# An eight-expert MLP behind an FFT filter: the seven products in another order, and transfers moved to ScalarE's queue

## The chip, the cores and the metric

The kernel runs on one core of one Trainium2 chip. The metric is the time of one execution in microseconds on the device. In the profile the engines are PE (TensorE, matmuls) with PEld (its weight loads), DVE (VectorE), ACT (ScalarE), POOL (GpSimd) and SP (SyncE, which issues transfers). A transfer is issued by an engine's queue, in that queue's order, and is then moved by the 16 DMA engines. `L808` is line 808 of the kernel before.

## The reference, cut to what matters

Two blocks follow each other. The first filters every one of 8 sequences of 2496 rows and 256 channels along the sequence; the second sends every row through one of eight two-layer networks, chosen by a hash of its token number.

```python
def _attn_ref(x, filt_r, filt_i):          # x: (8, 2496, 256)
    X = np.fft.rfft(x, axis=1)
    F = (filt_r + 1j * filt_i)[None, :, :]
    return np.fft.irfft(X * F, n=x.shape[1], axis=1).astype(np.float32)

def _moe_ref(x, token_ids, w1, w2):        # x: (19968, 256), w1: (8, 256, 1024), w2: (8, 1024, 256)
    expert_idx = token_ids * np.int64(2654435761) % np.int64(8)
    for e in range(8):
        mask = expert_idx == e
        h = np.maximum(x[mask] @ w1[e], 0.0)
        out[mask] = h @ w2[e]
```

All values are float32.

## The kernel before

**The filter.** The transform over 2496 = 39 x 64 points is done as two small transforms. A batch goes through four steps: `stage1` (L239) multiplies by a table over 39 points and writes a block to memory (`d1`), `load2` (L258) reads it back turned, `forward` (L266) does the second transform on PE and multiplies by the filter on DVE (tiles `y` and `z` from a pool of three buffers with the tag "p"), `back` (L285) transforms back and writes `d2`, `load4` (L362) reads that, and `stage3` (L367) ends the transform and scatters the finished rows with indirect transfers into a buffer `xs` in memory, ordered by expert. The writes of `d1` (L256) and `d2` (L301) are issued from POOL, except those of batch 2's `d1`, which are issued from ACT. The first two batches are handled in the head of the kernel in another way, on the chip alone.

**The tiles.** `xs` is cut into tiles of 256 rows, each belonging to one expert. There are 85 places for tiles; 80 (`NSURE`) are always computed, the last five only if the count of used tiles asks for it, behind a branch (`rest`, L902). With the given inputs the profile shows 80 down products (2560 matmuls of 32 each), so the five were not computed. A tile can start when all batches that may hold its rows are scattered; five stages (`STAGES`, after 2, 3, 4, 6 and 8 batches) say so, and the tiles start at 0, 10, 20, 30 and 50. A row of `xs` holds 256 channels and four words with its row number in the output.

**One tile** (`step`, L869) issues in this order: the load of the tile after next (`load`, L754: four transfers on SP, each of 64 channels, the last one a word wider so that the row number comes along); `numbers` (L769) for the next tile, four small copies on POOL that pick the row numbers out of the loaded rows; `weight_sums` (L792) for the next tile, four subtractions on POOL; the scatter of the last tile's results (`store`, L848, two indirect transfers on POOL); `up`; the next weights of the up product; the next tile's tokens, transposed and summed on DVE (`token_parts`, `token_sums`); then `down` (L836), 32 matmuls for the second layer, and its next weights. Between `up` and `down`, at three places within `down`, and after it, `run_until` issues the pieces of the filter for later batches that fall due, by a written list of times in units of a tile.

**`up` (L801)** forms the first layer with seven products of half size instead of eight, in three banks of PSUM, a, b and c. A product is four matmuls of 128 columns (eight records in the profile). The order is a, c, b, a, b, c, b, and a second or third product on a bank adds to what stands there. Sums that leave a bank are taken by DVE (`plus`, L815, 0.69 us) and by ACT (a copy of the first a, L819; relus, L812). A product that adds to b or c once more must wait until DVE has read the bank; each further product has its own reader.

**The head** counts tokens by expert (`count` to `experts`), and a list of times below zero sets its order. `weights` for tiles 0 and 1 go through SP at times -99 to -98.7; `begin` (L746) at -76 closes the head's work area and loads tiles 0 and 1, half of the transfers on SP and half on ACT. `blanks` works out, at -80, the places in `xs` that hold no token, and `pads` (L639) at 7.4 writes empty rows there: 14 indirect transfers (`NQP`) from one buffer of the pool with the tag "p".

Transfers from SP and ACT share eight completion counters, which the program gives out in turn, so that the issue of one waits until the one before it on its counter has landed. Indirect transfers and others from POOL have eight of their own.

Of the kernel before, what the change touches and what calls it, by code (L numbers as in the profile page):

```python
# [19 lines left out]
P = 128  # L20
# [14 lines left out]
SG = 4  # L35
# [18 lines left out]

XW = C // 4 + 2

# [63 lines left out]
def kernel(  # L120
# [60 lines left out]
    class Batch:  # L181
# [57 lines left out]
        def stage1(self, u):  # L239
# [7 lines left out]
            if half == 1:  # L247


                eng = nc.scalar if self.b == 2 else nc.gpsimd  # L250
                moves = self.parts(self.d1, self.t1, v)
                if self.b == 2 and v > 0:
                    put_off.extend(moves)
                    return
                for dram, chip in moves:
                    eng.dma_start(out=dram, in_=chip)  # L256

# [27 lines left out]
        def back(self, u):  # L285
# [12 lines left out]
            if u % half == half - 1:  # L298
                for p in range(2):
                    a0 = p * NS + SG * (u // half)  # L300
                    nc.gpsimd.dma_start(out=self.d2[:, a0:a0 + SG, :],  # L301
                                        in_=self.g[p:P:2, :, :])
# [94 lines left out]
    def weights(i, which):  # L397
# [3 lines left out]
        if i >= 2 and which == 0:  # L401
            ws[i] = ws[i - 2][0:2]
        eng, kw = nc.sync, {}
        if which == 0:
# [233 lines left out]

    def pads():  # L639
        blank = ppool.tile([P, 2 * C], I32, name="blank", tag="p")[:, 0:W]  # L640
        nc.vector.memset(blank[:, 0:C], 0)
        nc.vector.memset(blank[:, C:], N)
        for q in range(NQP):
            scatter(blank.bitcast(F32), at_i[:, q:q + 1], "xs_pad")
# [57 lines left out]
    todo += [(-154.2, count), (-152, route), (-150.9, later)]  # L702
    todo += [(-137.2, places), (-128, tile_experts), (-121, experts), (-80, blanks), (7.4, pads)]
    todo += [(t, lambda k=k: spread_filters(k)) for k, t in enumerate((-150.45, -146.6, -143, -137.6))]
# [8 lines left out]
    todo += [(t, lambda v=v: batches[2].load1(v)) for v, t in enumerate((-119, -117.5, -116))]  # L713
    todo += [(t, lambda u=u: batches[2].stage1(u)) for u, t in enumerate((-101.5, -99.5, -86, -85.5, -85, -84.5))]

    todo += [(-75.5, lambda: [nc.scalar.dma_start(out=dram, in_=chip) for dram, chip in put_off])]
    todo += [(t, lambda k=k: weights(k // 2, k % 2)) for k, t in enumerate((-99, -98.9, -98.8, -98.7))]
    todo += [(-76, lambda: begin())]

# [34 lines left out]
    def load(i):  # L754

        g = gath.tile([P, TB // 32, XW], F32, name=f"xg_{i}", tag="xg")
        rows = xs[tiles[i] * TB:(tiles[i] + 1) * TB, :]
        for q in range(4):
            w = C // 4 + (q == 3)
            ld = (nc.scalar if i < 2 and q % 2 else nc.sync).dma_start(  # L760
                out=g[32 * q:32 * q + 32, :, 0:w], in_=rows[:, 64 * q:64 * q + w].rearrange("(a t) c -> t a c", t=32))
            for b in range(STAGES[stage_of[i]], B):
                tc.declare_no_dep(ld.ins, group=f"xs_{b}", reason="the tiles of a stage hold tokens of its batches alone")
            if stage_of[i] < G - 1:
                tc.declare_no_dep(ld.ins, group="xs_pad", reason="places without a token lie in the last stage alone")
            tc.add_to_no_dep_group("xs_read", ld.ins)
        xg[i] = g

    def numbers(i):  # L769

        no = nums.tile([P, 2], I32, name=f"no_{i}", tag="no")
        for a in range(4):
            nc.gpsimd.tensor_copy(no[32 * a:32 * a + 32, :], xg[i][96:128, a::4, C // 4].bitcast(I32))  # L773
        to_rows[i] = no

# [24 lines left out]

    def up(i, ht):  # L801
        w1, x, st, t = ws[i][0], parts[i], parts[i]["sums"], sums[i]
        ps = {k: banks[k].tile([P, 4, P], F32, name=f"up_{i}_{k}", tag=k) for k in "abc"}
        h11, h12, h21, h22 = [ht[:, h, 4 * f:4 * f + 4, :] for h in range(2) for f in range(2)]

        def product(bank, w, xx, first):
            for f in range(4):
                nc.tensor.matmul(out=ps[bank][:, f, :], lhsT=w[:, f * P:(f + 1) * P], rhs=xx,  # L808
# [9 lines left out]
        product("a", w1[:, 0, 0:h], x[0, 0], True)  # L818
        nc.scalar.copy(out=h21, in_=ps["a"][:])  # L819
        product("c", t[0], st[:, 0, :], True)  # L820
        plus(h22, "c", h21)
        product("b", t[1], st[:, 1, :], True)
        plus(h12, "b", h21)
        product("a", w1[:, 1, 0:h], x[0, 1], False)
        relu(h11, ps["a"][:])
        product("b", t[2], st[:, 2, :], False)
        plus(h22, "b", h22)
        relu(h22, h22)
        product("c", w1[:, 1, h:], st[:, 3, :], False)
        plus(h12, "c", h12)  # L830
# [30 lines left out]
    weight_sums(0, nc.vector)  # L861
    numbers(0)
    used = []
# [5 lines left out]
    def step(i):  # L869
        ht = work.tile([P, 2, FP, P], F32, name=f"ht_{i}", tag="ht")  # L870
        if i + 2 < NT:
            load(i + 2)
        if i + 1 < NSURE:
            numbers(i + 1)
            weight_sums(i + 1)
        if i > 0:
            store(i - 1)
        up(i, ht)
        weights(i + 2, 0)
# [15 lines left out]
    for i in range(NSURE, NT):  # L895
        token_parts(i, mid[:, i - NSURE, 0:2 * TB].rearrange("p (d h t) -> p d h t", d=DP, h=2))
        numbers(i)
        if i + 2 < NT:
# [45 lines left out]
```

## Time and profile before

| | |
|---|---|
| median of 20 runs | 1554.39 us (1548.92 to 1558.11) |
| the profiled execution's own time | 1551.48 us |
| its span, from the first to the last instruction | 1549.8 us |
| mean granted TensorE clock | 0.969 |
| busy: PE, DVE, ACT, POOL | 1440.2, 807.2, 415.8, 894.9 us |
| longest waits: POOL's number copies (L773) | 80.9 us for out scatters, 74.5 for xs scatters, 44.5 for xg |
| POOL's writes of `d2` (L301) | 34.6 us of issue, 70.8 us of waits before them |
| POOL's writes of `d1` (L256) | 17.7 us of issue, 22.1 us of waits before them |
| number copies on POOL | 340, 64.2 us busy |

The profile is of one execution. Busy shares are means over stages with different limits: a head of about 165 us, a mixed part in which tiles and the filter of later batches alternate (to about 1069 us), a last part of tiles alone (to about 1525 us), and the end. A group's line gives the engine, the operation, what it writes and reads, how often, and its busy time; a wait's line says who waited for whom, how long in all, how often, and the longest. The matmuls' ends are modelled, so a product's cost is read from the start of one to the start of the next.

### The profile page before, as it was taken

To read this page: it belongs to the slowest core of one execution; us is meant where nothing else is said; L and a number is where in the kernel's file an instruction comes from. 1 tells how busy PE (TensorE), PEld (TensorE's weight loads), DVE (VectorE), ACT (ScalarE), POOL (GpSimd) and SP (SyncE) were. 2 spreads that over 40 slices of the span, in tenths; PEclk is the share of its full clock that TensorE was granted. 3 is DMA by queue.
4 is the path that set the end of the run, shared out by engine and by line. 5 is a ranking of instruction groups with operands and counts; after the bars stand their busy time and mean duration, and the time that the engine had idled before them with its cause. 6 is when DMAs were issued, how large, how long until landed. Compare 5 with 4: busy or idle time off the path is not lost.

```text
span 1549.8 us, 24884 instructions
## 1 busy us (share of the span) xinstructions
PE 1440.2 (93%) x8746; PEld 1296.6 (84%) x8746; DVE 807.2 (52%) x1362; ACT 415.8 (27%) x710; POOL 894.9 (58%) x1120
## 2 busy tenths in 40 slices
PE   6978799887999999999999999999999999999993
PEld 6966688776888888887998998988999999999993
DVE  6852563355456557434664456454454555545452
ACT  3543133222223323322233222222222222222220
POOL 5055436665556656657656677566765646465541
PEclk9998799898999999999999999999999999999997
DMA  8254666835897597797755653646513242332311
GB/s 225 64 179 125 176 198 184 254 110 179 254 262 233 161 286 217 236 272 250 225 159 145 181 165 112 153 132 195 150 47 112 67 123 65 99 92 69 106 42 38
DMA packets 201673, 245.73 MB, mean 159 GB/s; under 512 B 105749, under 2 KB 170701, under 8 KB 194426
## 3 DMA queue, kind: packets, MB, share of 16 engines
q1 hardware_dynamic: 168919, 166.72, 38.9%
q0 software_dynamic: 28480, 73.44, 14.5%
q10 hardware_dynamic: 4147, 3.95, 0.9%
q8 instruction: 72, 1.18, 0.3%
q14 instruction: 55, 0.45, 0.1%
HBM read 251.19 MB, written 75.14 MB: 211 GB/s over the span
## 4 chain that ended last, share of the span: by engine, by line
PE 78%; issue 6%; DMA 5%; DVE 5%; POOL 3%; another core or an unknown queue 1%; ACT 0%; SPq 0%; ACTq 0%; POOLq 0%; DVEq 0%
PE dps L841 31%; PE up_b L808 14%; PE up_c L808 8%; PE up_a L808 8%; PE pd L226 4%; PE pb L271 4%; PE pa L226 3%; PE pc L294 3%; DVE z L281 1%; DMA wts<-in_x_dram 1%; DMA xs<-o,sidx 1%; DVE ht L815 1%; POOL tw L798 1%; DMA mid<-d 1%
## 5 line engine op out<-in xcount | busy, mean ns | idle before, releaser
L841 PE MATMUL dps<-wts,ht 128*128 128x256 f32 x2560 | 582.5, 381 | 0.0
L841 PEld LDWEIGHTS dps<-wts,ht 128*128 128x128 f32 x2560 | 484.2, 191 | 66.6 <-issue 1.6
L815 DVE TENSOR_TENSOR ht<-up_b,ht 128x512 f32<-128x512 f32 x240 | 166.0, 692 | 173.1 <-PE up_b L808 134.7
L384 POOL DMA_INDIRECT xs<-o,sidx x176 | 178.1, 1012 | 128.6 <-issue 48.6
L798 POOL TENSOR_TENSOR tw<-wts 128x512 f32<-128x512 f32 x158 | 203.5, 1288 | 38.0 <-DMA wts<-in_moe_w_dram 32.1
L851 POOL DMA_INDIRECT out_dram<-osb,no x160 | 161.3, 1008 | 109.6 <-DVE osb L846 75.1
L798 POOL TENSOR_TENSOR tw<-wts,tw 128x512 f32<-128x512 f32 x158 | 204.1, 1292 | 6.2
L808 PE MATMUL up_b<-st,tw 128*128 128x128 f32 x1280 | 178.6, 284 | 31.0 <-DVE ht L815 30.6
L812 ACT ACTIVATE ht<-ht 128x512 f32<-128x512 f32 x240 | 151.1, 630 | 180.1 <-DVE ht L815 162.1
L808 PEld LDWEIGHTS up_b<-st,tw 128*128 128x128 f32 x1280 | 158.7, 195 | 43.0 <-POOL tw L798 16.7
L773 POOL COPY no<-xg 32x2 int32<-32x2 int32 x340 | 64.2, 189 | 224.6 <-DMA out_dram<-osb,no 80.9
L846 DVE COPY osb<-dps 128x512 f32<-128x512 f32 x80 | 55.4, 692 | 261.3 <-PE dps L841 226.5
L808 PE MATMUL up_a<-xt,wts 128*128 128x128 f32 x1280 | 171.3, 278 | 6.0 <-issue 6.0
L815 DVE TENSOR_TENSOR ht<-up_c,ht 128x512 f32<-128x512 f32 x160 | 110.6, 691 | 126.7 <-PE up_c L808 111.1
L808 PEld LDWEIGHTS up_a<-xt,wts 128*128 128x128 f32 x1280 | 164.0, 194 | 11.3 <-issue 7.3
L819 ACT COPY ht<-up_a 128x512 f32<-128x512 f32 x80 | 46.9, 587 | 350.4 <-PE up_a L808 340.3
L281 DVE TENSOR_TENSOR z<-pb,filt 64x512 f32<-64x512 f32 x160 | 110.2, 688 | 24.8 <-PE pc L294 22.8
L808 PE MATMUL up_b<-xt,tw 128*128 128x128 f32 x640 | 92.6, 289 | 9.2 <-DVE ht L815 7.0
L812 ACT ACTIVATE ht<-up_a 128x512 f32<-128x512 f32 x80 | 47.8, 597 | 197.0 <-PE up_a L808 146.4
L808 PEld LDWEIGHTS up_b<-xt,tw 128*128 128x128 f32 x640 | 79.8, 196 | 20.4 <-issue 10.3
L789 DVE TENSOR_TENSOR st<-xt 128x128 f32<-128x128 f32 x160 | 87.9, 550 | 2.8
L808 PE MATMUL up_c<-st,tw 128*128 128x128 f32 x640 | 85.6, 277 | 4.0 <-POOL tw L798 4.0
(145 smaller groups left out, 1483.7 us busy)
## 6 DMA issues: line engine op xcount, KB each, us to landing
wts<-in_moe_w_dram SPq DMA_DIRECT2D x162, 1024.0 KB
xg<-xs SPq DMA_DIRECT2D x253, 64.0 KB
mid<-d SPq DMA_DIRECT2D x60, 256.0 KB
d<-mid POOLq DMA_DIRECT2D x60, 256.0 KB
t<-d SPq DMA_DIRECT2D x12, 960.0 KB
x<-in_x_dram SPq DMA_DIRECT2D x36, 312.0 KB
d<-mid POOLq DMA_DIRECT2D x10, 960.0 KB
xg<-xs SPq DMA_DIRECT2D x83, 65.0 KB
```

Source lines behind the costliest of these rows:

```text
L226: nc.tensor.matmul(out=ps[0:cols * H, k, :], lhsT=w[:], rhs=src[:, 2 * i + k, :], start=True, stop=True)
L271: nc.tensor.matmul(out=ps[:, i, :], lhsT=d_t[:, s, :], rhs=rhs, start=True, stop=True)
L281: nc.vector.tensor_tensor(out=z[b], in0=ps[a], in1=f_t[1][64 * hi:64 * hi + 64, s1:s1 + 2, :], op=OP.mult)
L384: st = nc.gpsimd.indirect_dma_start(out=xs[:], out_offset=bass.IndirectOffsetOnAxis(ap=index, axis=0), in_=rows, in_offset=None, bounds_ch ...
L773: nc.gpsimd.tensor_copy(no[32 * a:32 * a + 32, :], xg[i][96:128, a::4, C // 4].bitcast(I32))
L789: nc.vector.tensor_tensor(st[:, k, :], p, q, op=op)
L798: eng.tensor_tensor(t[k][:], p, q, op=OP.subtract)
L808: nc.tensor.matmul(out=ps[bank][:, f, :], lhsT=w[:, f * P:(f + 1) * P], rhs=xx, start=first and f == 0, stop=True, skip_group_check=True)
L812: nc.scalar.activation(out=out, in_=in_, func=AF.Relu)
L815: nc.vector.tensor_tensor(out, ps[bank][:], other, op=OP.add)
L841: nc.tensor.matmul(out=ps[:, h, :], lhsT=ht[:, h, fp, :], rhs=w2[:, fp, :], start=(fp == 0), stop=(fp == FP - 1))
L851: st = nc.gpsimd.indirect_dma_start(out=out[:], out_offset=bass.IndirectOffsetOnAxis(ap=to_rows[i][:, h:h + 1], axis=0), in_=o[:, h, :], i ...
```

## The change

- `up` takes the seven products in the order a, b, c, half of a, b, the other half of a, c, b. The relu of a's sum is issued behind the relu of the b sum that precedes the second half of a. A hook `between`, behind the copy of the first a, issues the load of the tile after next.
- `load` takes four transfers of 64 channels and a fifth that brings the row numbers straight into their tile (256 elements of 4 bytes). `numbers` goes. Loads of tiles 0 and 1 are issued from SP, all others from ACT.
- The writes of `d1` and `d2` are issued from ACT for every batch.
- The empty rows are written in seven pairs, at times 10.9, 11.6, 11.9, 16.9, 17.6, 17.95 and 22.9, and their places are worked out at -90.
- In the head, weights for tiles 0 and 1 are issued from ACT at -101, -98, -95 and -92; `begin` moves from -76 to -84.9; four pieces of batch 2's `stage1` move from -86 to -84.5 up to -84.8 to -84.5, behind `begin`.

```diff
@@ stage1, back
-                eng = nc.scalar if self.b == 2 else nc.gpsimd
 ...
-                    eng.dma_start(out=dram, in_=chip)
+                    nc.scalar.dma_start(out=dram, in_=chip)
 ...
-                    nc.gpsimd.dma_start(out=self.d2[:, a0:a0 + SG, :],
+                    nc.scalar.dma_start(out=self.d2[:, a0:a0 + SG, :],
                                         in_=self.g[p:P:2, :, :])
@@ weights
-        eng, kw = nc.sync, {}
+        eng, kw = nc.scalar if i < 2 else nc.sync, {}
@@ pads
-    def pads():
-        blank = ppool.tile([P, 2 * C], I32, name="blank", tag="p")[:, 0:W]
+    def pads(k):
+        blank = ppool.tile([P, 2 * C], I32, name=f"blank_{k}", tag="p")[:, 0:W]
 ...
-        for q in range(NQP):
+        for q in (2 * k, 2 * k + 1):
@@ the list of times
-    todo += [(-137.2, places), (-128, tile_experts), (-121, experts), (-80, blanks), (7.4, pads)]
+    todo += [(-137.2, places), (-128, tile_experts), (-121, experts), (-90, blanks)]
+    todo += [(t, lambda k=k: pads(k)) for k, t in enumerate((10.9, 11.6, 11.9, 16.9, 17.6, 17.95, 22.9))]
 ...
-    todo += [(t, lambda u=u: batches[2].stage1(u)) for u, t in enumerate((-101.5, -99.5, -86, -85.5, -85, -84.5))]
+    todo += [(t, lambda u=u: batches[2].stage1(u)) for u, t in enumerate((-101.5, -99.5, -84.8, -84.7, -84.6, -84.5))]
 ...
-    todo += [(t, lambda k=k: weights(k // 2, k % 2)) for k, t in enumerate((-99, -98.9, -98.8, -98.7))]
-    todo += [(-76, lambda: begin())]
+    todo += [(t, lambda k=k: weights(k // 2, k % 2)) for k, t in enumerate((-101, -98, -95, -92))]
+    todo += [(-84.9, lambda: begin())]
@@ load, numbers
-        g = gath.tile([P, TB // 32, XW], F32, name=f"xg_{i}", tag="xg")
+        g = gath.tile([P, TB // 32, C // 4], F32, name=f"xg_{i}", tag="xg")
+        no = nums.tile([P, 2], I32, name=f"no_{i}", tag="no")
         rows = xs[tiles[i] * TB:(tiles[i] + 1) * TB, :]
-        for q in range(4):
-            w = C // 4 + (q == 3)
-            ld = (nc.scalar if i < 2 and q % 2 else nc.sync).dma_start(
-                out=g[32 * q:32 * q + 32, :, 0:w], in_=rows[:, 64 * q:64 * q + w].rearrange("(a t) c -> t a c", t=32))
+        moves = [(g[32 * q:32 * q + 32, :, :], rows[:, 64 * q:64 * q + 64].rearrange("(a t) c -> t a c", t=32))
+                 for q in range(4)]
+        moves.append((no[:].bitcast(F32), rows[:, C:C + 1].rearrange("(h p) c -> p (h c)", p=P)))
+        for to, src in moves:
+            ld = (nc.sync if i < 2 else nc.scalar).dma_start(out=to, in_=src)
 ...
-        xg[i] = g
-
-    def numbers(i):
-
-        no = nums.tile([P, 2], I32, name=f"no_{i}", tag="no")
-        for a in range(4):
-            nc.gpsimd.tensor_copy(no[32 * a:32 * a + 32, :], xg[i][96:128, a::4, C // 4].bitcast(I32))
-        to_rows[i] = no
+        xg[i], to_rows[i] = g, no
@@ up
-    def up(i, ht):
+    def up(i, ht, between=lambda: None):
 ...
-        def product(bank, w, xx, first):
-            for f in range(4):
+        def product(bank, w, xx, first, fs=range(4)):
+            for f in fs:
 ...
         product("a", w1[:, 0, 0:h], x[0, 0], True)
         nc.scalar.copy(out=h21, in_=ps["a"][:])
+        between()
+        product("b", t[1], st[:, 1, :], True)
+        plus(h12, "b", h21)
         product("c", t[0], st[:, 0, :], True)
         plus(h22, "c", h21)
-        product("b", t[1], st[:, 1, :], True)
-        plus(h12, "b", h21)
-        product("a", w1[:, 1, 0:h], x[0, 1], False)
-        relu(h11, ps["a"][:])
+        product("a", w1[:, 1, 0:h], x[0, 1], False, (0, 1))
         product("b", t[2], st[:, 2, :], False)
         plus(h22, "b", h22)
         relu(h22, h22)
+        product("a", w1[:, 1, 0:h], x[0, 1], False, (2, 3))
+        relu(h11, ps["a"][:])
         product("c", w1[:, 1, h:], st[:, 3, :], False)
@@ step
-        if i + 2 < NT:
-            load(i + 2)
         if i + 1 < NSURE:
-            numbers(i + 1)
             weight_sums(i + 1)
         if i > 0:
             store(i - 1)
-        up(i, ht)
+        up(i, ht, lambda: load(i + 2) if i + 2 < NT else None)
```

More of the change, by code (lines that the diff above doesn't have):

```diff
@@ L53 @@
 NSURE = NT - 5
-XW = C // 4 + 2
 def stage_tiles():
@@ L861 @@
     weight_sums(0, nc.vector)
-    numbers(0)
     used = []
@@ L896 @@
         token_parts(i, mid[:, i - NSURE, 0:2 * TB].rearrange("p (d h t) -> p d h t", d=DP, h=2))
-        numbers(i)
         if i + 2 < NT:
```

## The prediction

> **What bounds the kernel now.** I read the page first, then the table of stretches (length, busy time and instructions of PE, PEld, DVE, ACT and POOL, granted clock, DMA share, GB/s), the timeline of one tile in the last stage, the waits, and the timelines around the longest TensorE waits (start, length, engine, and in brackets the idle time before). The lines, in the order of the argument:
>
> ```profile
> span 1549.8 us, 24884 instructions
> ```
>
> ```profile
> 165.00:1069.00 904.00, 856.60 (x5054) 766.49 (x5053) 474.50 (x791) 245.10 (x423) 557.30 (x677) 0.98 0.67 198
> 1069.00:1525.00 456.00, 456.00 (x2938) 418.26 (x2938) 234.44 (x365) 103.12 (x169) 260.66 (x334) 1.00 0.32 90
> ```
>
> ```profile
> 1307.69 1.05 PE L808 MATMUL up_a<-xt,wts 128*128 128x128 f32 x8
> ...
> 1309.48 1.06 PE L808 MATMUL up_b<-st,tw 128*128 128x128 f32 x8
> ...
> 1310.37 1.06 PE L808 MATMUL up_a<-xt,wts 128*128 128x128 f32 x8
> 1310.57 0.69 DVE L815 TENSOR_TENSOR ht<-up_b,ht 128x512 f32<-128x512 f32 x1
> ...
> 1311.41 1.13 PE L808 MATMUL up_b<-st,tw 128*128 128x128 f32 x8
> ...
> 1312.37 1.06 PE L808 MATMUL up_c<-st,wts 128*128 128x128 f32 x8
> ...
> 1313.41 1.13 PE L808 MATMUL up_b<-xt,tw 128*128 128x128 f32 x8
> ...
> 1314.27 6.78 PEld L841 LDWEIGHTS dps<-wts,ht 128*128 128x128 f32 x32
> 1314.38 7.07 PE L841 MATMUL dps<-wts,ht 128*128 128x256 f32 x32
> ```
>
> ```profile
> 333.40 1.25 POOL L384 DMA_INDIRECT xs<-blank,at_i  x1 [0.30 <-DVE z L281]
> ...
> 353.02 0.69 DVE L277 TENSOR_TENSOR y<-pb,filt 128x512 f32<-128x512 f32 x1 [14.03 <-DMA xs<-blank,at_i]
> ...
> 357.94 2.04 PE L808 MATMUL up_b<-st,tw 128*128 128x128 f32 x8 [15.81 <-DVE ht L815]
> ```
>
> ```profile
> 154.58 13.05 SPq L208 DMA_DIRECT2D x<-in_x_dram  x6
> ...
> 156.37 1.85 ACTq L760 DMA_DIRECT2D xg<-xs  x4
> ...
> 660.94 11.63 SPq L760 DMA_DIRECT2D xg<-xs  x4
> ...
> 1538.84 0.84 POOL L773 COPY no<-xg 32x2 int32<-32x2 int32 x4 [1.62 <-DMA xg<-xs]
> ```
>
> TensorE is the bound. From 1069 us on it is busy all of the time at clock 1.00, a tile taking 13.60 us; before that it is busy 856.60 of 904 us. Busy hides small holes, so the tile has to be read by starts. A product that nothing delays takes 0.89 to 0.90 us to the next one's start (1309.48 to 1310.37). The seven take 1314.38 - 1307.69 = 6.69 us where 7 x 0.895 = 6.27 were due. The 0.43 us lie at two places: a to the third product on b takes 1.04, and c to the fourth on b 1.04, each b itself 0.96. There the bank is added to again, and VectorE must first have read it: its sum starts 0.20 after the product's end, takes 0.69, and TensorE goes on 0.15 later (1311.26 to 1311.41). Read and restart need 1.04 us; one product between covers 0.895. That happens in all 80 tiles.
>
> **The change part by part.** The sum is made against the profiled execution, 1551.5 us (span 1549.8 and 1.7 around it). The median of the runs, 1554.4, stands 2.9 higher, which I add at the end.
>
> *Order of the products.* It is now a, b, c, half a, b, half a, c, b. Between b's uses lie one and a half products, 1.34 us against the 1.04 needed; c has two and more. Both holes go: 80 x 0.43 = -34.9 (0.436 by the unrounded starts). What is late next is the first quarter of the down product: its relu used to follow the second a at once, and now stands on ScalarE behind the relu of the b sum. With the tile's start as zero, b's second use ends at 4.5 x 0.895 = 4.03; VectorE's sum runs 4.23 to 4.92, the first relu 4.96 to 5.59 (0.63), the relu of a to 6.19 (0.60). The down product's weight load is due 0.11 before its matmul (1314.27, 1314.38), at 6.265 - 0.11 = 6.155, and a signal takes 0.05 to 0.15. So it is 0.09 to 0.19 late; I take 0.13, 80 x 0.13 = +10.4. Ends for the pair: -34.9 (no lateness) to 0 (a lateness as large as the old holes). Sum -24.5.
>
> *Empty rows in pairs.* Fourteen scatters, 1.29 us apart, hold one of the three buffers that the filter's outputs y and z rotate through; VectorE waits 14.03, TensorE 15.81. Pairs hold POOL 2.6 us, at places where no batch is in its filter. The 15.97 of lost start-to-start time go, and the clock's loss with them: the stretch 350 to 360 us has a granted clock of 0.50, 360 to 370 of 0.87, and the 24 matmuls after the stall take 5.0 us for 2.7. That is -18.3; at the least -14, if each pair still holds y back half a microsecond. The Trainium skill (TensorE: Matmul & The Clock Gate, Part 1: The HAM clock gate) says that the array runs at half rate for its first 3.4 us or so of work after an idle window; by that alone the loss after the stall would be 1.7 us, an estimate, where the rows give 2.3. The measurement is what I use.
>
> *Row numbers by transfers.* POOL loses 340 copies (64.2 us busy) and their waits (80.9 on the out scatters, 74.5 on the xs scatters, 44.5 on xg). Most of that is off the path. On it lie the two holes that end with POOL's weight sums, 0.55 and 3.45 us at 697 and 736, with 1.7 of half clock after the second: -6, between 0 (the sums are late for the scatters' sake anyway) and -8. The added transfer is 256 elements of 4 bytes per tile. The hardware queue's 168,919 packets took 38.9% of 16 engines' span, 57 ns each, so 256/16 x 57 = 0.9 us of the engines per tile; a DMA share of 0.32 (last stage) to 0.67 hides it: 0. At share 0.96 (400 to 440 us) the cover is gone and it would be up to 0.9 in a few tiles.
>
> *Loads on ScalarE's queue, from inside the up product.* 83 tiles x 5 issues move from SP to ACT, behind the copy of a (ends 1.74 in the tile's time) and ahead of the relu due at 4.96: 3.2 us of room. A load's issue is 0.46 us (1.85 for four), so five take 2.3, and the room holds. Two things can break it. First, every transfer of SP and ACT takes the next of eight completion counters in the built program and waits for the landing of the one before on it. In eight tiles (2, 3, 16, 22, 25, 30, 31, 37) a load so waits for the next tile's down weights, which SP can only issue as this tile starts. One megabyte at the 260 GB/s of the busiest stretch is 4 us, 5 with the issue: the last issue ends at 5.7 instead of 4.0, the relu 0.75 late. Where transfers crowd it may be 3.7 late. I take 1.5 x 8 = +12 (6 to 30). Second, an issue can take longer: on SP the same four loads took 11.63 us at 660.94, directly behind a weight load. Over the 47 groups from 178 to 1078 us, 25 exceed 2.73 (3.2 less one issue), by 65 us together. The only such row on ACT's queue took 1.85 while SP stood 13.05 us over six x loads. Bounds 0 to +65; ACT's own row is nearest, so +5. What queues behind a held load: all relus, and the evacuations of the other batches' matmuls.
>
> The Trainium skill (DMA: Bandwidth & Descriptors, Issuing engines are not separate DMA queues) speaks against this part: transfers started on several engines run on the same 16 engines, and only issue time is saved. By it SP's backlog would stay with the loads, and the whole +65 would stand instead of +5. No run here shows loads of xg on ACT beside the weights.
>
> *Block rows and stores on ACT.* 80 stores leave POOL (52.3 us of issue, 92.9 of waits before them) for ACT, 0.37 to 1.35 us each (131.30: 0.37; 158.32: 4.05 for three). ACT is busy 245 of 904 us there; its idle time hides them: 0, up to +10 where one holds a copy.
>
> *Head.* Weights 0 and 1 go to ACT: six issues and their register loads, about 4.8 us, while POOL waits for ACT twice (6.82 and 2.21). Tile 0's loads all go to SP: two of its four stood on ACT until 156.37, so tokens come 2.8 us sooner. But TensorE then waits at 177.01 for block rows that SP issues at 173.12, behind the x loads, now behind five more transfers. Empty-row places ten steps earlier: 2.3 us of VectorE with no reader. Together 0, from -5 to +5.
>
> *Tail.* POOL's last copy ends 1539.68, and the span 10.1 later. POOL would now end at 1528.64, with VectorE's last transposes about 2.3 sooner than 1539.58. If the ending follows POOL, -10; if it follows the last of all, -2.3. I take the middle, -6.
>
> Sum: -24.5 - 18.3 - 6 + 12 + 5 - 6 = -37.8. 1551.5 - 37.8 = 1513.7; plus 2.9, **1517 us**.
>
> **The rivals.** *Slower: ACT's issues are held as SP's were* (0.18). For: the row at 660.94, and the shared counters. Against: the ACT row of 1.85. Price +65 in place of +5: 1517 + 60 = 1577. It decides from a mean hold of (37.8 + 5)/47 = 0.9 us per tile of the mixed stages. *The relu takes the place of the bank* (0.16): the down product waits 0.43 instead of 0.13, the order brings nothing, 1517 + 24.5 = 1541. For: 6.19 against 6.155; against: the starts allow only 0.2. *Nothing is held at all* (0.13): order -34.9, no ACT terms, tail -10: 1517 - 10.4 - 17 - 4 = 1486. *The gains and the holds cancel within 0.2%* (0.03).
>
> **How the numbers follow.** Forecast 0.50, the rivals as given. Faster than before by over 0.2%, about what a measurement of this kernel can tell: 0.50 + 0.16 + 0.13 = 0.79; slower 0.18; same 0.03. The range must leave out 2 in 10 at most: from 1488, just above the lowest case, up to 1566, inside the slower one.
>
> **What would show it.** Right: seven products in 6.3 to 6.45 us in the last stage, no 1.04 step before b, a small one before dps; no wait of y on blank; L773 gone; ACT's groups of five loads near 2.3 us. Wrong: groups on ACT's queue longer than 3.2 us, followed by relus that start late and a dps that waits for ht; or load2 of batch 2 landing later than 177.

## The result, and the profile after

| | before | changed |
|---|---|---|
| median | 1554.45 us | 1508.09 us (1506.62 to 1518.61) |
| profiled execution: span | 1549.8 us | 1505.9 us |
| first product of the first tile | 162.0 us | 157.7 us |
| end of the last product | 1525.4 us | 1493.2 us |
| from there to the end | 24.4 us | 12.7 us |

The changed kernel takes 0.9708 of the time before, 95% interval 0.969 to 0.9725: 46.4 us less by the medians, where 37.8 were forecast. It is faster, and inside the range. The sum behind the number is another matter: several of its terms were wrong by more than 10 us, in both directions.

The page of the changed kernel, its first line, and the table of stretches (length, busy time and instructions of PE, PEld, DVE, ACT, POOL, granted clock, DMA share, GB/s) for the mixed part and the part of tiles alone:

```profile
span 1505.9 us, 24354 instructions
```

```profile
157.70:1058.70 901.00, 855.90 (x5100) 769.94 (x5101) 481.73 (x814) 237.17 (x427) 476.10 (x424) 0.98 0.66 200
1058.70:1493.20 434.50, 434.46 (x2905) 406.81 (x2903) 242.49 (x359) 97.75 (x165) 224.55 (x193) 1.00 0.32 91
```

In the last part TensorE is still busy all of the time; the part is shorter because a tile is. One tile of it in the timeline (start, length, engine; in brackets the idle time before), TensorE and then ScalarE:

```profile
1321.91 1.05 PE L802 MATMUL up_a<-xt,wts 128*128 128x128 f32 x8
1322.81 1.06 PE L802 MATMUL up_b<-st,tw 128*128 128x128 f32 x8
1323.70 1.06 PE L802 MATMUL up_c<-st,tw 128*128 128x128 f32 x8
1324.59 0.61 PE L802 MATMUL up_a<-xt,wts 128*128 128x128 f32 x4
1325.04 1.06 PE L802 MATMUL up_b<-st,tw 128*128 128x128 f32 x8
...
1328.16 7.07 PE L837 MATMUL dps<-wts,ht 128*128 128x256 f32 x32
1335.07 0.38 PE L802 MATMUL up_a<-xt,wts 128*128 128x128 f32 x2
```

```profile
1323.06 0.59 ACT L813 COPY ht<-up_a 128x512 f32<-128x512 f32 x1 [6.50 <-PE up_a L802]
1323.16 1.81 ACTq L762 DMA_DIRECT2D xg<-xs  x4
1325.09 0.39 ACTq L762 DMA_DIRECT2D no<-xs  x1
1326.86 0.63 ACT L806 ACTIVATE ht<-ht 128x512 f32<-128x512 f32 x1 [3.21 <-DVE ht L809]
1327.40 0.58 ACT L806 ACTIVATE ht<-up_a 128x512 f32<-128x512 f32 x1
```

The seven products take 1328.16 - 1321.91 = 6.25 us (6.69 before), and the tile 1335.07 - 1321.91 = 13.16 instead of 13.60. Every step is 0.89 to 0.90, each half of a 0.45; both holes are gone and no new one stands ahead of dps. The load's five issues end at 1325.48, 1.4 us ahead of the relu: here the room holds.

In the mixed part it does not. The waits of TensorE and of ScalarE (who waited for whom: us in all, times, longest):

```profile
PE dps L837 <- ACT ht L806: 22.2, 8, 9.3
```

```profile
ACT ht L806 <- DMA xg<-xs: 140.4, 31, 12.9
ACT ht L806 <- DMA no<-xs: 23.1, 7, 3.5
```

In 38 places the profile names a load's transfer as the last thing that ScalarE waited for ahead of a relu, 163.5 us of idle time in all. About 3.2 us of each is idle time in the plain tile too (the 3.21 above, for VectorE's sum), so the holds themselves made the relus late by 42 us or so. The down product waited 22 us for a relu, a wait that the kernel before did not have. The worst place, tile 18, in the timeline:

```profile
529.67 7.37 SPq L260 DMA_DIRECT2D mid<-d  x2
...
533.23 0.58 ACT L813 COPY ht<-up_a 128x512 f32<-128x512 f32 x1 [6.57 <-PE up_a L802]
533.56 7.30 ACTq L762 DMA_DIRECT2D xg<-xs  x4
...
537.46 1.06 PE L802 MATMUL up_b<-xt,tw 128*128 128x128 f32 x8
...
546.26 0.38 ACTq L762 DMA_DIRECT2D no<-xs  x1
546.69 0.63 ACT L806 ACTIVATE ht<-ht 128x512 f32<-128x512 f32 x1 [12.87 <-DMA xg<-xs]
547.22 0.58 ACT L806 ACTIVATE ht<-up_a 128x512 f32<-128x512 f32 x1
...
547.85 1.65 PE L837 MATMUL dps<-wts,ht 128*128 128x256 f32 x3 [9.33 <-ACT ht L806]
```

Five issues take 13.1 us. By the completion counters in the trace four of them wait for two t loads and two mid loads of SyncE's queue, and TensorE stands for 9.3 us until the second relu is done.

POOL, in turn, has time to spare. Its longest waits, changed kernel (before, they were the number copies' waits for transfers):

```profile
POOL tw L792 <- DMA wts<-in_moe_w_dram: 183.2, 41, 18.6
POOL out_dram L847 <- DVE osb L842: 170.1, 36, 12.3
```

It now waits 183 us for weights, 32 before: the weight sums are ready as soon as their weights are.

**A ledger by tile.** Take the time from a tile's first product to the next tile's, and subtract the length of a tile in the last part of the same kernel (13.59 before, 13.16 changed). What is left is filter work and holes, and can be compared across the two orders:

| tile | before | changed | difference |
|---|---|---|---|
| 8 (empty rows) | 26.51 | 8.64 | -17.87 |
| 27 (late weight sums) | 9.03 | 3.45 | -5.58 |
| 43 to 46 | 12.27 | 6.66 | -5.61 |
| 6 and 19 | 29.15 | 17.08 | -12.07 |
| 4, 13, 18, 26, 29, 30 | 41.15 | 75.06 | +33.91 |
| all others | | | +14.06 |
| sum over the mixed part | | | +6.84 |

With 80 x 0.435 = -34.8 for the order, -4.3 for the earlier first tile and -11.7 at the end this gives the -43.9 of the spans. The order and the empty rows are worth 53 us; the rest of the mixed part gave 24.7 of them back. Of the six tiles that became longer, 4, 18, 29 and 30 (25.0 us together) lost it at held loads: with the loads back on SyncE, below, all four are as short as in the kernel before, to 0.3 us. Tiles 13 and 26 (8.9 us) hold waits of ScalarE and VectorE, 5.2 and 3.9 us, whose releaser the profile calls "remote"; on the third chip, where no such wait is shown, the changed kernel does not lose these 8.9 us.

### The profile page after: what moved, and what is told of

It is laid out like the page before. It is cut to its first block, busy times and chain, and to the rows that moved or that the text cites. A ratio compares the mean times of both kernels' runs of the same rounds, so it can differ in the third digit from the quotient of the medians.

```text
span 1505.9 us, 24354 instructions
## 1 busy us (share of the span) xinstructions
PE 1412.6 (94%) x8746; PEld 1284.0 (85%) x8746; DVE 819.4 (54%) x1374; ACT 401.4 (27%) x710; POOL 773.3 (51%) x700
## 4 chain that ended last, share of the span: by engine, by line
PE 79%; DMA 9%; issue 7%; DVE 3%; ACTq 1%; ACT 1%; another core or an unknown queue 1%; POOL 0%; SPq 0%; DVEq 0%; POOLq 0%
PE dps L837 35%; PE up_b L802 13%; PE up_a L802 8%; PE up_c L802 8%; PE pb L269 4%; PE pc L292 3%; PE pd L225 3%; PE pa L225 3%; DMA xg<-xs 2%; DMA mid<-d 1%; DMA wts<-in_x_dram 1%; DMA t<-d 1%; DVE z L279 1%; DMA wts<-in_moe_w_dram 1%; DMA d_t<-d_tbl 1%
## 5 line engine op out<-in xcount | busy, mean ns | idle before, releaser
L837 PE MATMUL dps<-wts,ht 128*128 128x256 f32 x2560 | 588.6, 383 | 22.2 <-ACT ht L806 22.2
L806 ACT ACTIVATE ht<-ht 128x512 f32<-128x512 f32 x240 | 149.5, 629 | 342.4 <-DVE ht L809 165.9
L802 PE MATMUL up_a<-xt,wts 128*128 128x128 f32 x1280 | 185.0, 278 | 12.0 <-issue 8.2
L802 PEld LDWEIGHTS up_a<-xt,wts 128*128 128x128 f32 x1280 | 170.2, 194 | 17.7 <-issue 8.6
L802 PE MATMUL up_b<-st,tw 128*128 128x128 f32 x1280 | 172.7, 279 | 4.7 <-DVE ht L809 3.7
L809 DVE TENSOR_TENSOR ht<-up_c,ht 128x512 f32<-128x512 f32 x160 | 110.5, 691 | 65.3 <-PE up_c L802 43.9
L783 DVE TENSOR_TENSOR st<-xt 128x128 f32<-128x128 f32 x160 | 99.5, 622 | 2.8
L275 DVE TENSOR_TENSOR y<-pb,filt 128x512 f32<-128x512 f32 x80 | 55.2, 690 | 64.7 <-PE pb L269 52.7
L802 PE MATMUL up_b<-xt,tw 128*128 128x128 f32 x640 | 85.3, 276 | 3.5 <-DVE ht L809 3.5
L802 PE MATMUL up_c<-st,wts 128*128 128x128 f32 x640 | 85.9, 278 | 0.4 <-issue 0.4
L802 PE MATMUL up_c<-st,tw 128*128 128x128 f32 x640 | 84.5, 275 | 0.0
```

The source lines that it names most:

```text
L783: nc.vector.tensor_tensor(st[:, k, :], p, q, op=op)
L806: nc.scalar.activation(out=out, in_=in_, func=AF.Relu)
L809: nc.vector.tensor_tensor(out, ps[bank][:], other, op=OP.add)
L837: nc.tensor.matmul(out=ps[:, h, :], lhsT=ht[:, h, fp, :], rhs=w2[:, fp, :], start=(fp == 0), stop=(fp == FP - 1))
```

## The experiments

The kernels named b_ are the kernel before with one part of the change; those named a_ are the changed kernel with one part undone or moved. Three chips ran them, and the kernel before took 1554.9, 1534.5 and 1536.9 us there, so times are compared within a chip and ratios to the kernel before across chips. The changed kernel's first figures (1508.09 beside 1554.45) go with the first chip's by the time of the kernel before.

### The order alone

```diff
 (kernel before; loads stay on SyncE at the start of the step)
         nc.scalar.copy(out=h21, in_=ps["a"][:])
+        product("b", t[1], st[:, 1, :], True)
+        plus(h12, "b", h21)
         product("c", t[0], st[:, 0, :], True)
 ... the rest of up as in the change, without the hook
```

> The kernel before with the new order of the seven products and nothing else; the loads stay on SyncE. By the trace of the changed kernel a tile of the last stage lost 13.60 - 13.16 = 0.435 us and the down product follows without a hole, so the order should be worth the whole 80 x 0.435 = 34.8 us: 1554.5 - 34.8 = 1519.7. As the prediction had it (relu of a late by 0.13 us a tile): 1554.5 - 24.5 = 1530. If the relu comes in time only because something else in the changed kernel moved (a freer POOL or VectorE), a tile would take 13.3 us or more here. A second question: the waits of 7.4 us in tile 6, 4.6 in tile 19 and 5.6 in tiles 43 to 46, which the changed kernel lost besides. If the order removes them, 1502 to 1510; if they belong to POOL's number copies, they stay and 1520 it is.

Measured: 1534.7 us, ratio 0.9852 (0.9803 to 0.9901): -20.2 us by the medians. That is nearest to the forecast's own -24.5, for another reason than the forecast gave. A tile of the last part takes 13.16 us, the whole 34.8 are there. But the first tile starts 4.0 us later, and tiles 0, 25 to 27 and 44 became longer by 3.7, 6.1 and 3.2; in tile 44 VectorE waits 3.9 us for "remote". The waits of TensorE and the timeline at tile 27 show the largest of these:

```profile
PE up_b L808 <- POOL tw L798: 9.1, 3, 5.0
```

```profile
739.05 1.22 POOL L773 COPY no<-xg 32x2 int32<-32x2 int32 x4 [3.37 <-DMA xs<-o,sidx]
740.35 1.26 POOL L798 TENSOR_TENSOR tw<-wts 128x512 f32<-128x512 f32 x1
741.68 1.26 POOL L798 TENSOR_TENSOR tw<-wts,tw 128x512 f32<-128x512 f32 x1
742.90 1.26 POOL L798 TENSOR_TENSOR tw<-wts 128x512 f32<-128x512 f32 x1
743.00 0.71 PEld L808 LDWEIGHTS up_b<-st,tw 128*128 128x128 f32 x3 [5.18 <-POOL tw L798]
```

POOL's number copies stand ahead of the weight sums in POOL's order and wait there for a scatter of x rows; faster tiles only arrive earlier at the same late sums. That explains the 6.1 us of tiles 25 to 27, out of 16.0 that the mixed part gave back; the rest is spread over other tiles and not explained.

### The empty rows in pairs alone

```diff
 (kernel before)
-    (7.4, pads)
+    todo += [(t, lambda k=k: pads(k)) for k, t in enumerate((10.9, 11.6, 11.9, 16.9, 17.6, 17.95, 22.9))]
 ... pads(k) as in the change
```

> The kernel before with the empty rows written in seven pairs at the new times, and nothing else. Theory: the wait of 15.97 us and the half clock after it go, 18 us in all: 1554.5 - 18 = 1536. Rival: each pair holds a buffer of y and z somewhere else, or delays POOL's weight sums, and the gain is given back in part: 1540 to 1554.

Measured: 1558.9 us, ratio 1.0026 (0.9999 to 1.0053): nothing gained, which is worse than both expectations. Tile 8 lost exactly what it lost in the changed kernel, 26.51 to 8.64. Tile 25 gave 11.2 back, behind the last pair at 22.9:

```profile
696.79 0.85 POOL L774 COPY no<-xg 32x2 int32<-32x2 int32 x4 [6.05 <-DMA xs<-o,sidx]
697.72 1.26 POOL L799 TENSOR_TENSOR tw<-wts 128x512 f32<-128x512 f32 x1
699.03 1.14 PEld L809 LDWEIGHTS up_c<-st,tw 128*128 128x128 f32 x5 [10.66 <-POOL tw L799]
```

Again it is a number copy that waits, and the weight sums behind it. Tile 13 gave back 6.9 and tile 19 2.5, both at waits of ScalarE (in tile 19 of VectorE as well) whose releaser the profile calls "remote", which other kernels on that chip have at other places; those may not belong to the pairs.

### The row numbers alone

```diff
 (kernel before; loads on SyncE, the fifth with them)
+        moves.append((no[:].bitcast(F32), rows[:, C:C + 1].rearrange("(h p) c -> p (h c)", p=P)))
-    def numbers(i): ...
-            numbers(i + 1)
```

> The kernel before with the row numbers brought by a fifth transfer per tile (on SyncE's queue), POOL's number copies gone, nothing else. Theory: POOL's copies, which wait for other engines' data at the head of POOL's queue, are what made the weight sums late in tiles 25 and 27 (6.5 us), what lay behind the waits of tiles 6, 19 and 43 to 46 (17.6 us, gone in the changed kernel, and not gone with the order alone or the pairs alone), and what set the end (11.7 us): 1554.5 - 36 = about 1519. As the prediction had it: -6 for the sums and -6 for the end, 1542. Rival: the copies only fill time in which POOL would wait anyway: the end alone, 1543 to 1549.

Measured: 1496.86 us against 1534.49 on that chip, ratio 0.9753 (0.9722 to 0.9783): -37.6 us, for the part that the forecast put at -6 and the end's -6. It alone brings most of what the whole change brings (0.9708). From the end of the products to the end of the kernel it takes 15.5 us instead of 24.4, and tiles 24 to 27 leave 12.4 us over the plain tile instead of 21.5. For the other 20 us there is no profile of the kernel before on that chip to subtract, so they are not divided here, and that late weight sums took them is not shown.

### The numbers, the stores, and both, back on POOL

```diff
 a_numbers_pool (changed kernel)
-        moves.append((no[:].bitcast(F32), ...))
+    def numbers(i): ...            # four copies on POOL, called ahead of weight_sums
 a_stores_pool (changed kernel)
-                    nc.scalar.dma_start(out=dram, in_=chip)           # d1
+                    (nc.scalar if self.b == 2 else nc.gpsimd).dma_start(out=dram, in_=chip)
-                    nc.scalar.dma_start(out=self.d2...
+                    nc.gpsimd.dma_start(out=self.d2...
 a_both_pool: the two together
```

> The changed kernel with the row numbers taken off the fourth load by POOL's copies again, as before. Theory: POOL falls behind once more, and with tiles that come faster than before by more: 11.7 at the end, 6 to 20 in the weight sums of tiles 24 to 28, and the waits of tiles 6, 19 and 43 to 46 back: 1535 to 1550. As the prediction had it: 1508 + 12 = 1520. One issue less on ScalarE's queue would give back a few us in either case.

> The changed kernel with the writes of d1 and d2 issued from POOL again. Theory: POOL waits 183 us for weights in the changed kernel and so has room; the stores cost nothing on either queue, 1504 to 1513. Rival 1: not the copies but the 80 stores and the waits ahead of them made POOL late: 1520 to 1535, with the weight sums as the releaser of the up products. Rival 2: on ScalarE the stores' issues stand among the held loads; without them ScalarE's holds shrink: 1490 to 1503.

> The changed kernel once more, as the yardstick for the three others on their chip, because the chip of the last four ran the kernel before at 1534 us and the first one at 1555. If chips differ only by a factor, the ratio to the kernel before is 0.971 again. If the chips differ in how long transfers take, the changed kernel, whose relus stand behind held loads, gains more on a faster one: 0.955 to 0.965.

> The changed kernel with the number copies and the block stores both back on POOL; order, pairs, loads on ScalarE's queue and the head stay. Theory: either of the two alone leaves POOL enough room, both together make its weight sums late for tiles that now come faster: 20 to 35 us over the yardstick, with the weight sums as the releaser of the up products in tiles 19 to 28 and 43 to 47, and the longer end. Rival: POOL's load never cost more than the 6 us that the prediction read from two holes, plus the end: 6 to 12 over the yardstick. If fewer issues on ScalarE's queue outweigh that: below the yardstick.

Measured, as ratios to the kernel before: numbers back 0.9717 (0.9685 to 0.9749), stores back 0.9685 (0.9649 to 0.9721), both back 0.984 (0.9808 to 0.9871); the changed kernel 0.9708, and 0.9703 (0.967 to 0.9737) on the chip of the last. So my expectation for the numbers was wrong: by the total, either part alone can be undone at no cost that shows, and both together cost 1511.31 - 1489.65 = 21.7 us. But the total of the numbers hides a price and a relief of nearly the same size. TensorE's waits with the numbers alone back:

```profile
PE up_b L808 <- POOL tw L798: 19.0, 7, 5.1
```

Against the changed kernel on the third chip, tiles 7, 25, 27 and 47 are 25.9 us longer, and the end takes 21.6 us instead of 12.6. The other tiles are 26.4 shorter: with one issue less in each group, the groups of loads on ScalarE's queue pass their room (3.2 us, less one issue here) by 19 us instead of 60, and TensorE waits 5.5 us for relus instead of 23.3. With the stores alone back, the groups pass it by 39 us, the mixed part is 9.0 us shorter and the end 3.2 longer. These are single profiles on two chips; the spans lie 7.5 us apart with the numbers back, where the medians lie 2.0. TensorE's waits in the kernel with both back:

```profile
PE up_b L808 <- POOL tw L798: 32.8, 11, 5.1
...
PE dps L843 <- ACT ht L812: 1.2, 1, 1.2
```

With both, POOL is late again (tiles 7, 18, 20, 24, 25, 27), 32.8 us; with the numbers alone back it is late in fewer places (above all in tiles 7, 25 and 27), with the stores alone back in none over 0.5 us. The changed kernel itself, run again as a yardstick, kept its ratio, so a chip with a faster kernel before does not favour it. The second line shows the other side: with fewer issues on ScalarE's queue, the down product hardly waits for a relu.

### The loads on SyncE, and behind the relus

```diff
 a_loads_sp (changed kernel)
-            ld = (nc.sync if i < 2 else nc.scalar).dma_start(out=to, in_=src)
+            ld = nc.sync.dma_start(out=to, in_=src)
 step
+        if i + 2 < NT:
+            load(i + 2)                     # at the start of the step
-        up(i, ht, lambda: load(i + 2) if i + 2 < NT else None)
+        up(i, ht)
 a_loads_late (changed kernel): still on ScalarE, load(i + 2) directly behind up(i, ht)
```

> The changed kernel with the five loads of a tile issued from SyncE at the start of the step, as the kernel before did with four. Theory: the holds of the loads on ScalarE's queue delay the relus and so the down product, which in the tile-by-tile ledger against the kernel before cost about 45 us in tiles 0 to 31; they go, and SyncE's own holds cost little: 1508 - 45 + 5 = about 1468 (1463 to 1485). Rival: the transfers crowd each other wherever they are issued from, and tiles wait for the same data: 1500 to 1512.

> The changed kernel with the five loads still on ScalarE's queue, but issued behind the last relu of the up product instead of behind the copy of the first product. Theory: no relu of this tile stands behind a held load any more; what stands there are evacuations of other batches' products and, where a hold lasts over 7 us, the next tile's copy. So most of the 45 us go: 1470 to 1490. Rival, as above: 1500 to 1512. If the evacuations matter as much as the relus, above 1500 as well, and then the waits of TensorE name pa, pc and pd instead of dps.

Measured on one chip: from SyncE 1490.45 us, ratio 0.9575 (0.9531 to 0.9618), 17.6 under the changed kernel; behind the relus 1516.01 us, 0.9743 (0.9701 to 0.9784), 8 over it. The first says that the place of the issue matters, not the transfers alone; it gained less than I expected: in tile 12 SyncE issued a t load behind the load group and four mid loads, at 404.67, and TensorE waited 6.2 us for it; tiles 15 and 35 lost 4 each, with VectorE's sums as the releaser. VectorE itself had waited 4.1 and 3.7 us for "remote" there, and tiles 19 and 26 lost 6.0 us beside such waits, so the 17.6 us are not a clean price. SyncE's groups of loads were also held longer than ScalarE's had been, by 149 us over 3.2 us a group where it was 55. The edit moves the issue to the start of the step as well as to another queue; the two are not told apart here. The second missed. ScalarE's waits show why:

```profile
ACT o L227 <- DMA xg<-xs: 40.0, 10, 9.5
ACT mid L295 <- DMA xg<-xs: 21.7, 10, 3.0
ACT ht L813 <- DMA xg<-xs: 13.8, 2, 7.1
```

The relus are free, but now the evacuations of the filter's products (o, mid) stand behind the held issues. That kernel also waits 16.7 us at VectorE for "remote" (3.9 in the changed kernel's profile), so the 8 us are not a clean price.

### The old order in the changed kernel

```diff
 (changed kernel; the hook stays behind the first copy)
-        product a, b, c, half a, b, half a, c, b
+        product a, c, b, a, b, c, b         # as before
```

> The changed kernel with the old order of the seven products; the load's hook stays behind the first copy. Theory: the order is worth 0.435 us a tile in all 80 tiles once POOL keeps up: 1508 + 34.8 = 1543. As the prediction had it: 1508 + 24.5 = 1532.5. Rival: the old order gives the relus more room behind a held load, and lost holds cover part of it: 1525 to 1535.

> The changed kernel with the old order of the products, now on one chip with its yardstick. Theory: the order is worth 0.435 us in each of 80 tiles: 34.8 us over the yardstick. As the prediction had it: 24.5. Rival: the old order leaves the relu of a ahead of the relu of the b sum and so suffers less from held loads: 13 to 22 over the yardstick.

Measured: 1503.12 us, ratio 0.9807 (0.9776 to 0.9839), on the second chip; beside the changed kernel on the third 1500.35 against 1489.65, ratios 0.9759 (0.9729 to 0.9789) and 0.9703 (0.967 to 0.9737). Undone, the order costs 10.7 us, below the rival's 13 to 22 and far below 34.8. The tile of the last part is 13.60 again, so 34.8 us do come back; the mixed part is 18.8 us shorter in the ledger of the two profiles (these two executions lie 17.9 us apart, where the medians lie 10.7). TensorE's waits for relus in these two, first the changed kernel, then with the old order:

```profile
PE dps L837 <- ACT ht L806: 23.3, 10, 9.4
```

```profile
PE dps L836 <- ACT ht L806: 7.6, 5, 2.9
```

In the old order the relu of a, the one that the down product's first matmul needs, is the first thing behind the load; in the new one it is the second, and the tile has 0.43 us less slack. In tile 18 of the two orders the hold itself also differs, 13.1 us against 6.4: when the load is issued decides which transfers it meets. Why it differs by so much is not settled.

### Loads on SyncE and stores on POOL

This takes up what the others point to: nothing but the head's transfers and batch 2's first stores stays on ScalarE's queue.

```diff
 (a_loads_sp and a_stores_pool together)
```

> The changed kernel with the loads on SyncE's queue (the experiment that gained 17.6 us) and the block stores back on POOL, so that nothing but batch 2's first stores and the head's weights is left on ScalarE's queue. Theory: no relu and no evacuation stands behind a transfer's issue any more, and POOL has room for the stores once the number copies are gone: 18 to 28 us under the yardstick, the fastest of all. Rival: SyncE, which then has all loads, delays the other batches' block rows and weights, and POOL's stores come late: 5 to 15 under the yardstick.

Measured: 1447.42 us against 1489.65 for the changed kernel and 1536.86 for the kernel before on that chip: ratio 0.9415 (0.9385 to 0.9446), 42 us under the changed kernel, more than the 18 to 28 that I expected. Page, table of stretches and ScalarE's waits:

```profile
span 1445.9 us, 24372 instructions
```

```profile
154.60:1000.00 845.40, 839.64 (x5139) 762.23 (x5140) 478.14 (x818) 242.85 (x428) 535.11 (x509) 1.00 0.71 214
```

```profile
ACT ht L806 <- DVE ht L809: 302.7, 240, 6.2
```

In the mixed part TensorE is busy 839.64 of 845.40 us (855.90 of 901.00 in the changed kernel), at clock 1.00. The 240 relus of VectorE's sums now wait for VectorE alone. The ledger against the changed kernel on the same chip is -41.3 us over the mixed part, 11.6 of them in tile 18; the end is 3.2 longer. SyncE's load groups are still long (62 us over 3.2 us a group, 60 on ScalarE's queue in the changed kernel): the holds are not gone, but on SyncE they hold nothing that TensorE waits for.

## Why the prediction was right or wrong

The direction, the range and the order of size were right. That the likeliest time was right to 9 us is luck: terms that were too small on both sides cancelled.

| term of the sum | forecast | found |
|---|---|---|
| both holes of the product order | -34.9 | -34.8 |
| relu of a late | +10.4 | 0 in the last part; part of the holds in the mixed part |
| empty rows | -18.3 | -17.9 in tile 8; nothing in all when done alone |
| row numbers | -6 | with the end, -37.6 alone; undone alone, nothing in the total: 19.0 of waits and 9.0 at the end, against shorter holds |
| loads on ScalarE's queue | +17 | 17.6 with the stores on ScalarE too (first chip); about 41 with the stores on POOL (0.9685 to 0.9415, across two chips) |
| stores on ScalarE | 0 | undone alone 0.9685 against 0.9708: not resolved; undone with the numbers back, or with the loads moved, much |
| head | 0 | not tried by itself |
| end | -6 | -11.7: undone, the numbers cost 9.0 there and the stores 3.2 |

- **The order.** The reading by starts, 0.435 us at two places in 80 tiles, was right to the tenth, and so was the claim that one and a half products cover 1.04 us.
- **"The relu of a to 6.19."** This step failed. In the tile shown the relu of a ends at 1327.98 - 1321.91 = 6.07. I added the two relus' lengths, 0.63 and 0.60; but the second starts at 1327.40, 0.54 after the first, while that one is still shown busy until 1327.49. The Trainium skill (Perfetto Trace Analysis, Optimizing Scalar/DVE Operations) says that a profiled latency includes the write's acknowledgement, which overlaps with the next instruction; this trace shows the overlap, 0.09 us, though not what it consists of. Durations of neighbours on ScalarE must not be summed: the starts must be used, as I did for TensorE.
- **The empty rows.** -17.87 in tile 8 against 18.3: the wait of 15.97 and 1.9 of half clock, between the 1.7 of the rule and the 2.3 of the rows that the prediction set side by side. What I left out is that the gain needs a POOL that keeps up: in the kernel before, the last pair pushed a number copy and the weight sums behind it, 11.2 us.
- **"Most of that is off the path" (row numbers).** This step failed most. I priced the copies by the two holes that they made in the kernel before, 6 us. But 200 us of waits stood ahead of the weight sums in POOL's order, so POOL had little slack, and part of each gain elsewhere ended at late weight sums: 6.1 us of the order's 34.8, 11.2 of the pairs' 17.9. The numbers alone gained 37.6, about 9 of it at the end and 9 in tiles 24 to 27; where the other 20 lie stays open. In the changed kernel two parts give POOL its room, numbers and stores. Without the numbers it is late again, 19.0 us of TensorE's waits and 9.0 at the end, but the holds on ScalarE's queue shrink by about as much; without both, the price shows in the total, 21.7 us.
- **Loads on ScalarE.** The rival's mechanism came true, beside the gains: issues on ScalarE's queue are held as SyncE's were. By the measure of the prediction (a load's five issues over 3.2 us) there are 23 groups and 55 us, where SyncE had 25 and 65. "ACT's own row is nearest, so +5" was the wrong choice: one row of 1.85 us was a case with free counters. My list of eight tiles counted only waits for down weights, and missed the t, mid and x loads. What the rival had wrong is the price, 60 more than forecast: only part of a hold reaches TensorE. Moving the loads away gained 17.6 us on the first chip with the stores left on ScalarE, and about 41 with the stores on POOL (0.9685 to 0.9415, across two chips). In the first of these, four tiles with "remote" waits lost 13.9 us, and SyncE's groups were held longer (149 us against 62); how much of the difference is the stores' and how much the chips' is not told apart. Against the kernel before the holds took 25 us in four tiles of the ledger, more than the 17, and so gave back about half of what the order and the pairs brought. The Trainium skill's rule (DMA: Bandwidth & Descriptors, Issuing engines are not separate DMA queues), which I weighed against the trace and set aside, was nearer for the length of the holds: they moved with the transfers. No fixed length moved, though: with the stores off ScalarE's queue the same groups were held 39 us.
- **End.** "If the ending follows POOL, -10" was the case: -11.7. Taking the middle of two cases was wrong where one of them could be read from the order of POOL's last instructions.
- **Head.** The first tile started 4.3 us earlier and was 1.8 longer. With the head of before, on the first chip, the first tile starts anywhere from 158.9 to 165.9 in three profiles, so the profile does not resolve it. On the second chip the row numbers alone, with the old head, start their second tile at 175.5 and the changed kernel with the old order at 180.1: there the new head looks 4.6 us worse, by one profile each.
- **What else went.** Tiles 6 and 19 lost 12 us that I had not forecast. In these tiles of the kernel before VectorE and ScalarE wait for "remote", and such waits occur at other tiles in other kernels of that chip; I do not count them for the change. Since the ratio is the same on a chip without them (0.9703), they did not decide the result. The 5.6 us of tiles 43 to 46 went with neither the order alone nor the pairs alone. They are not there with the numbers alone, on the second chip (6.4 us over the plain tile against 12.3 before). With both POOL parts back, on the third chip, tiles 43 to 45 are free and tiles 46 and 47 lose 5.3 us beside late weight sums. What held them in the kernel before stays open.

## What to carry to other kernels

Before pricing a part by the holes it makes now, ask which engine will be late once the other parts are in: an engine whose queue is full of waits (POOL's number copies, 200 us) can take back part of other gains, and relief for it may be worth several times its visible holes. Do not put transfers whose issue can be held on an engine that evacuates or activates for TensorE: groups of loads held for 60 us over their room made TensorE wait 23.3 us for relus on ScalarE's queue, and with 62 us on SyncE's, and the stores off ScalarE too, no such wait is left and the kernel is 42 us faster. And when a bundle comes out near the forecast, undo its parts singly and in pairs, and read the waits of each as well as the total: undoing the numbers alone seemed free, because a price of 28 us (19.0 of waits, 9.0 at the end) was nearly made good by shorter holds. Here moving two parts back gained 42 us, and that version took 0.9415 of the time before instead of 0.9703.

## What the runs showed that was not expected

- Two activations that follow each other on ScalarE are shown 0.63 and 0.58 us long but start 0.54 apart.
- On one of three chips the profile has waits of VectorE and ScalarE of up to 10 us released by "remote", in every kernel (VectorE's sums in the kernel before, four waits):

```profile
DVE ht L815 <- remote: 12.1, 4, 6.4
```

On the other two chips no kernel shows one, and the kernel before is 18 to 20 us faster there (1534.5 and 1536.9 against 1554.9). What they are is open.
- Taking one part at a time does not add up to the change: the parts taken alone measure -20 (order), 0 (pairs) and -38 (numbers, with their end, on another chip); the whole is -46, with the holds in it.
